# Score projection as 64x128 tiles on two row halves, four PSUM banks a round

## The chip, the cores and the metric

The kernel runs on one core of one Trainium2 chip. The time is the device time of one execution in microseconds; the kernel before took 1718.86 us, the median of three runs (1711.59 to 1719.67). In the profile, PE is the tensor engine (PEld its weight loads), DVE the vector engine, ACT the scalar engine, POOL the GpSimd engine and SP the engine that here issues DMAs and executes no-ops.

## The reference

The input is one sequence of 2048 tokens of 448 numbers. Two layers run over it, each an attention and a feed-forward part with a residual addition, all with the same weights:

```python
x = x + attention(layernorm(x))      # layer one
x = x + feed_forward(layernorm(x))
x = x + attention(layernorm(x))      # layer two
x = x + feed_forward(layernorm(x))

# attention: 64 segments of 32 tokens, one after the other, 16 heads of 256
mem = mem0                                        # 8 rows
for s in range(64):
    h = concat(mem, x[32 * s:32 * s + 32])        # 40 rows of 448
    q, k, v = h Wq, h Wk, h Wv                    # for each head
    p = softmax(mask(q k^T / 16))
    o = sum over heads of (p v) Wo
    mem = o[:8]                                   # goes into the next segment
    out[s] = o[8:]

# feed_forward: relu(x W_gate) * (x W_up), then W_down; 448 -> 1792 -> 448
```

The memory rows make the segments of one attention a chain: segment s + 1 can't start before segment s has its output.

## The kernel before

**Folded weights.** At the start `score_weights` multiplies Wk and Wq of each head into one 448 x 448 matrix, so that the scores of a head are h M h^T. It lies in `M_sb` (the first 384 of the 448 contracted rows, as three blocks of 128 partitions) and `MT_sb` (the last 64 rows). `value_weights` folds Wv and Wo in the same way into `B_sb` and `BT_sb`.

**Two chains.** Layer one (chain C1) and layer two (C2) run interleaved, C2 five segments behind (`LAG`). There are 69 steps; step g does segment g of C1 and segment g - 5 of C2. So 59 steps hold both chains and ten hold one. The activations are kept transposed in `hTr`: slots 0 to 2 hold 128 rows each, slots 3 and 4 both stand for the last 64 rows. Slot 3 has them in partitions 0 to 63 and zeros below, slot 4 in partitions 64 to 127 and zeros above.

**A step**, in the order in which PE gets it:

1. The score projection G = M^T h (L320 to L337). It has 56 column tiles of 128, and 40 columns of h for each chain, so 80 with both. For each tile four matmuls follow one another, three on `M_sb` and one on `MT_sb`, each a full 128 x 128 array. `MT_sb` holds two heads' tails, one in each half of the partitions, and the zeros in slot 3 or 4 switch the other off. Six tiles fill a PSUM bank; ACT and DVE take turns in copying a bank to G (L333).
2. The scores (L353) in `S_ps`, which has two banks of its own. The first half of its matmuls reads tiles 0 to 27 of G, the second half tiles 28 to 55.
3. The softmax on DVE and ACT (L358 to L374), while PE multiplies the memory and token rows by the folded value weights (`values`, L265). `values` works already on 64 x 32 tiles of two row halves: each half fills its own banks, and a no-op on SP (L268) holds half 0 back from a bank that half 1 is still adding to.
4. The weighted sum (`AT_ps`, L421), its memory rows copied to `mb` (L427), transposed (L163) and put into `hTr` for the next step (L434, L435); last, the tokens' rows are added to the residual in `x_ring` (L446, one addition for each chain).

**PSUM.** All other tiles come from `bank`, which hands out six banks in turn. A tile's first writer waits until the bank's last reader is done:

```python
n_bank[0] += 1
return psum.tile(shape, dt, tag=f"b{n_bank[0] % 6}", name=name)
```

**The order around it** is written by hand. A plan for each step (chosen by g mod 4, called r) puts pieces of other work at named places: G0, G4, G6 and G9 in and behind the projection, P behind the softmax weights' transposes, A, B and T behind the weighted sum. A block of 128 tokens is normalized (`Norm`) once four segments of it are done, transposed (`turn`), and its feed-forward goes into a queue of seven `gate_up` blocks of 16 matmuls and one `down`. `fill` takes from that queue; the elementwise ends of the blocks wait in `owed` until `settle()` or a later `fill` puts them out. With r = 0 layer one's feed-forward runs seven blocks at G9 (between projection and scores) and `down` at P; layer two's blocks are spread over P, B and T of the next steps. Stores and reloads of `x_ring` are put off to the start of a later step (`deferred`), on SP's queue.

Of the kernel before, what the change touches and what calls it, by code (L numbers as in the profile page):

```python
# [10 lines left out]
F32 = mybir.dt.float32  # L11
# [5 lines left out]
DM = 448  # L17
# [3 lines left out]
NGT = 56  # L21
# [3 lines left out]
L = MEM + SEG  # L25
# [17 lines left out]
def build_kernel(ctx, tc, A_x, A_mem0, A_Wq, A_Wk, A_Wv, A_Wo, B_W_gate, B_W_up, B_W_down, out,  # L43
                 ntiles=16, nseg=64):
    nc = tc.nc
    P = nc.NUM_PARTITIONS
# [20 lines left out]
    M_sb = glob.tile([P, 3, H * DM], BF)  # L67
    MT_sb = glob.tile([P, H * DM // 2], BF)
# [7 lines left out]
    def bank(shape, dt, name):  # L76

        n_bank[0] += 1
        return psum.tile(shape, dt, tag=f"b{n_bank[0] % 6}", name=name)
# [78 lines left out]
    def transposed(xn, rows):  # L158

        tps = bank([P, NSL, P], BF, "tps")  # L160
        for kd in range(NSL):
            lo = 320 if kd == 4 else kd * 128
            nc.tensor.transpose(tps[:, kd, 0:rows], xn[0:rows, lo:lo + 128], ident[0:rows, 0:rows])  # L163
        return tps

    def prep_x(c, blk, tps):

        src = tps[:, :, :].rearrange("p k (s t) -> p s k t", t=SEG)
        s0 = (4 * blk + c.lag) % NR
        for a, b in ([(0, 4)] if s0 + 4 <= NR else [(0, NR - s0), (NR - s0, 4)]):  # L170
            r = slice((s0 + a) % NR, (s0 + a) % NR + b - a)
            nc.vector.tensor_copy(hTr[:, r, 0:4, c.cid, 0:SEG], src[:, a:b, 0:4])
            nc.scalar.copy(hTr[64:128, r, 4, c.cid, 0:SEG], src[64:128, a:b, 4])

    def set_mem0(c):
        r = c.lag % NR
        nc.vector.tensor_copy(hTr[:, r, :, c.cid, SEG:L], mem0T[:])  # L177
        lo = SEG - 2 * MEM + MEM * c.cid
        nc.gpsimd.tensor_copy(memTp[c.lag % 2][:, :, lo:lo + MEM], mem0T[:])
# [4 lines left out]
    def settle():  # L184

        while owed:
            owed.pop(0)()
# [55 lines left out]
    def fill(cid, n):  # L243
        for _ in range(n):
            if ffn_q[cid]:
                while len(owed) > 1:
                    owed.pop(0)()
                ffn_q[cid].popleft()()

    def after(later, earlier):  # L250
        tc.add_manual_dep(later.ins, earlier.ins.name, SYNC, reason="one row half leaves a bank before the other enters")

    def values(lhsT, dst, evac, between=lambda: None):
# [24 lines left out]
        for slot in range(14):  # L278
            for r in range(2):
                chunk(r, *order[r][slot])  # L280
            if slot in (10, 13):
                for g4 in ((0, 1) if slot == 10 else (2, 3)):
                    evac[g4](dst[:, g4, :], ps[g4][:, 0:DM])  # L283
                if slot == 10:
                    between()

    prev_vom = [None]
    cp_a = nc.scalar.copy
    cp_v = nc.vector.tensor_copy
# [12 lines left out]
    def step(g, plan):  # L302

        chains = [c for c in (C1, C2) if 0 <= g - c.lag < nseg]
        both = len(chains) == 2
        rg = g % NR
        c0, c1 = chains[0].cid, chains[-1].cid + 1
        NP = L * (c1 - c0)
# [3 lines left out]
        hT = hTr[:, rg]  # L312

        def at_place(name):
            for f in plan.get(name, []):
                f()
# [1 line left out]
        for _ in range(len(deferred)):  # L318
            deferred.popleft()()
        G = p_vo.tile([P, NGT, 2, L], BF, tag="G", name="G")  # L320
        per_bank = 480 // NP
        for bb, t0 in enumerate(range(0, NGT, per_bank)):
            n = min(per_bank, NGT - t0)
            ps = bank([P, 512], F32, "gps")
            for t in range(t0, t0 + n):
                p7, u = divmod(t, 7)
                q7 = 7 * (p7 // 2) + u
                for kd in range(4):
                    w = M_sb[:, kd, t * 128:(t + 1) * 128] if kd < 3 else MT_sb[:, q7 * 128:(q7 + 1) * 128]
                    nc.tensor.matmul(ps[:, (t - t0) * NP:(t - t0 + 1) * NP], w,  # L330
                                     hT[:, kd if kd < 3 else 3 + p7 % 2, c0:c1, :],
                                     start=(kd == 0), stop=(kd == 3))
            (cp_a if bb % 2 == 0 else cp_v)(  # L333
                G[:, t0:t0 + n, c0:c1, :], ps[:, 0:n * NP].rearrange("p (m c t) -> p m c t", m=n, t=L))
            if bb == 0:
                settle()
            at_place(f"G{(t0 * 80 // 480)}" if both else f"G{bb * 2}")  # L337
        at_place("G9" if not both else "-")
        settle()

        S_ps = S_next[0] if S_next[0] is not None else mask_scores(g)
# [1 line left out]
        for bb in range(2):  # L343
            r4 = slice(4 * bb, 4 * bb + 4)
            for sl in range(NSL):
                for c in chains:
                    o = S_ps[c.rb:c.rb + L, bb, 0:8 * L].rearrange("p (r e k) -> p r e k", e=2, k=L)
                    if sl < 3:
                        rhs = Gv[:, r4, sl:sl + 5:4, c.cid, :]
                    else:  # L350
                        rhs = Gv[:, r4, 3, c.cid, :]
                        o = o[:, :, sl - 3, :]
                    nc.tensor.matmul(o, hT[:, sl, c.cid, :], rhs, start=False, stop=(sl == NSL - 1),  # L353
                                     tile_position=(0, c.rb), skip_group_check=True)
# [5 lines left out]
        nc.vector.tensor_tensor(se[RR].rearrange("p (b h) k -> p b h k", b=2), S3,  # L360
                                mx[RR].unsqueeze(3).to_broadcast([nr, 2, 8, L]), op=ALU.subtract)
        nc.scalar.activation(se[RR], se[RR], AF.Exp, scale=SCALE)  # L362
        ssum = p_soft.tile([P, H], F32, tag="ssum")
        rs = p_soft.tile([P, H], F32, tag="rs")
        Px, Pm = PXM[g % 2]
# [51 lines left out]
        for k in range(8):  # L417
            for c in chains:
# [3 lines left out]
                                 start=(k == 0), stop=(k == 7), tile_position=(0, c.rb), skip_group_check=True)  # L422
        at_place("A")
        nxt = [c for c in chains if g + 1 - c.lag < nseg]
        for c in nxt:
            rows = slice(c.rb + SEG, c.rb + L)
# [26 lines left out]
    def load_T(n, i, tag):  # L453
        t = bp.tile([P, 8, DM], BF, tag=tag, name=f"w{n}")
        nc.sync.dma_start_transpose(t[:], srcs[n][:, 1024 * i:1024 * (i + 1)])
        return t
# [3 lines left out]
    def copy_out(dst, src):  # L460
        flip[0] ^= 1
        if flip[0]:
            nc.scalar.copy(dst, src)
        else:
            nc.vector.tensor_copy(dst, src)

    def product(dst, lt, rt, hh, lo, n):
        for t in range(2):
            nc.tensor.matmul(dst, lt[:, 2 * hh + t, lo:lo + n], rt[:, 2 * hh + t, :],  # L469
                             start=(t == 0), stop=(t == 1))  # L470

    def store_M(dst, odd, ps):
        if not odd:
            copy_out(dst[:, 0:448], ps)
        else:
            copy_out(dst[:, 512:896], ps[:, 0:384])
            copy_out(dst[:, 448:512], ps[:, 384:448])

    def score_weights():
        for i in range(4):  # L480
            wk = load_T("k", i, "wa")
            wq = load_T("q", i, "wb")
            for hh in range(4):
                o = 896 * ((4 * i + hh) // 2)
                for mt in range(3):
                    ps = bank([P, 512], F32, "wps")
                    product(ps[:, 0:DM], wk, wq, hh, 128 * mt, 128)
                    store_M(M_sb[:, mt, o:o + 896], hh % 2, ps[:, 0:DM])
            for e in range(2):
                ps = bank([P, 512], F32, "wps")  # L490
                for side in range(2):
                    product(ps[64 * side:64 * side + 64, 0:DM], wk, wq, 2 * side + e, 384, 64)
                store_M(MT_sb[:, 896 * i:896 * i + 896], e, ps[:, 0:DM])

    def value_weights():
        for i in range(4):
# [32 lines left out]
    for t in range(2):  # L529
        prep_x(C1, t, transposed(Norm(t).apply(), P))  # L530
    nc.gpsimd.tensor_copy(memTp[0][:, :, 0:16], hTr[:, 1, :, 0, 0:16])
    score_weights()

    for g in range(nsteps):
        gb, r = divmod(g, 4)
        if g == LAG:
            set_mem0(C2)
        plan = {}
        hold = {}

        def put(place, f):
            plan.setdefault(place, []).append(f)

        def norm_at(key, t, first, second):
            put(first, lambda: hold.__setitem__(key, Norm(t)))
            put(second, lambda: hold.__setitem__(key, hold[key].apply()))

        if r == 0:
            if 0 <= gb - 1 < ntiles:
                f1 = FFN(C1, gb - 1)  # L550
                norm_at("f", gb - 1, "G0", "G4")
                put("G6", lambda: f1.turn(hold["f"]))
                put("G9", lambda: fill(0, 7))
                put("P", lambda: fill(0, 1))
                put("P", settle)
                norm_at("c2", gb - 1, "P", "A")
                put("B", lambda: hold.__setitem__("c2", transposed(hold["c2"], P)))
                put("B", lambda: prep_x(C2, gb - 1, hold["c2"]))
            put("B", lambda: fill(1, 1))
        elif r == 1:  # L560
            if 0 <= gb - 2 < ntiles:
                f2 = FFN(C2, gb - 2)
                norm_at("f", gb - 2, "G0", "G4")
                put("G6", lambda: f2.turn(hold["f"]))
            for place in "PBT":
                put(place, lambda: fill(1, 1))
        elif r == 2:
            if gb + 2 < ntiles:
                norm_at("c1", gb + 2, "G0", "G4")
                put("G6", lambda: prep_x(C1, gb + 2, transposed(hold["c1"], P)))  # L570
            for place in "BT":
                put(place, lambda: fill(1, 1))
        else:
            for place in "PB":
                put(place, lambda: fill(1, 1))
        step(g, plan)
    fill(0, 20)
    fill(1, 20)
# [61 lines left out]
```

## Time and profile before

| | |
|---|---|
| median of three runs | 1718.86 us |
| the profiled execution | 1715.13 us, span 1713.4 us |
| mean granted clock of TensorE | 0.992 |
| PE busy | 1634.1 us, 95% |
| DVE, ACT, POOL busy | 988.0, 633.0, 138.3 us |
| projection matmuls (L330) | 15456, 202 ns each with 80 columns |
| G copied by ACT | 559 ns for 480 columns, 426 ns for 320 |
| G copied by DVE | 651 ns for 480 columns, 325 ns for 160 |
| DMA | 28.83 MB, 17 GB/s |

A matmul's duration in the profile holds its way through the array, and matmuls overlap; what one costs in a run is the distance between two starts. In a list of groups a row is: line, engine, operation, tile written <- tiles read, shape and count, then busy time and mean duration, then idle time before it and what ended it. In a timeline a row is: start, time until the end of the merged rows, engine, line and operation, count, and the idle time before it with what ended it. In a table of windows, each engine has its busy time and the count of its instructions, then come the granted clock, the share of DMA and GB/s.

The set-up takes the first 47 us, the first step with both chains starts its projection at 181 us. From there on steps of one kind agree: from projection to projection 32.4 us with r = 0, 21.3 with r = 1, 22.7 with r = 2 and 20.2 with r = 3 (medians).

### The profile page before, as it was taken

What the parts mean: (1) busy time and instruction counts of PE and PEld (TensorE: products, weight loads), DVE (VectorE), ACT (ScalarE), POOL (GpSimd) and SP (SyncE); (2) the same over time, 40 slices, a digit from 0 to 9 for tenths busy, and PEclk for the clock granted to TensorE, in tenths of its full rate; (3) what the DMA queues carried; (4) which work ended last, traced back from release to release, by engine and by line L of the source; (5) the groups of instructions that cost most, each with busy time, mean ns of one, the idle gap of its engine ahead of it and who ended that gap; (6) DMA issues with size and microseconds to landing.
All of it is one profiled execution on the core that took longest, in us unless ns stands there. A gap on an engine that the chain in (4) does not pass through costs nothing.

```text
span 1713.4 us, 88473 instructions
## 1 busy us (share of the span) xinstructions
PE 1634.1 (95%) x41883; PEld 1252.6 (73%) x41883; DVE 988.0 (58%) x1916; ACT 633.0 (37%) x1365; POOL 138.3 (8%) x373
## 2 busy tenths in 40 slices
PE   5889999999999999999999999999999999999998
PEld 2457677777778787777778777787778777787775
DVE  4534556655665656655665556555566556555544
ACT  3423333333334333333334343333333343333332
POOL 1000001000000000000000000010000000010000
PEclk9989999999999999999999999999999999999999
DMA  8730000000000000000000000000000000000000
GB/s 186 175 115 3 3 3 4 4 3 9 3 9 3 6 6 6 7 3 9 3 9 4 6 7 6 6 3 9 3 9 4 6 4 6 4 3 7 3 7 8
DMA packets 55259, 28.83 MB, mean 17 GB/s; under 512 B 44008, under 2 KB 54000, under 8 KB 54896
## 3 DMA queue, kind: packets, MB, share of 16 engines
q1 hardware_dynamic: 54880, 23.17, 5.4%
q8 instruction: 327, 5.36, 1.3%
q14 instruction: 36, 0.29, 0.1%
q10 hardware_dynamic: 16, 0.01, 0.0%
HBM read 10.33 MB, written 1.84 MB: 7 GB/s over the span
## 4 chain that ended last, share of the span: by engine, by line
PE 86%; DVE 8%; ACT 2%; issue 1%; DMA 1%; POOL 1%; SPq 0%; POOLq 0%; ACTq 0%
PE gps L330 31%; PE vps L265 21%; PE gu L209 10%; PE AT_ps L421 7%; PE dps L224 5%; PE S_ps L353 5%; PE tps L163 3%; PE wps L469 2%; DVE Px L370 2%; PE PT_ps L409 2%; DVE mb L427 2%; ACT mb L427 2%; DVE ssum L373 1%; PE S_ps L296 1%; DVE Pm L370 1%
## 5 line engine op out<-in xcount | busy, mean ns | idle before, releaser
L330 PE MATMUL gps<-hTr,M_sb 128*128 128x80 bf16 (+1 forms) x11592 | 546.7, 199 | 0.9 <-DVE hTr L177 0.7
L330 PEld LDWEIGHTS <-M_sb 128*128 128x128 bf16 x11592 | 538.3, 100 | 10.4 <-issue 8.9
L330 PE MATMUL gps<-hTr,MT_sb 128*128 128x80 bf16 (+1 forms) x3864 | 538.7, 199 | 2.6 <-issue 2.6
L330 PEld LDWEIGHTS <-MT_sb 128*128 128x128 bf16 x3864 | 384.7, 100 | 2.7 <-issue 2.7
L333 ACT CAST G<-gps 128x480 bf16<-128x480 f32 (+1 forms) x325 | 180.4, 555 | 367.5 <-PE gps L330 367.5
L265 PE MATMUL vps<-B_sb,hTr 64*32 64x448 bf16 x9216 | 275.2, 349 | 1.0 <-issue 0.7
L333 DVE CAST G<-gps 128x480 bf16<-128x480 f32 x315 | 184.2, 590 | 142.0 <-PE gps L330 140.9
L265 PEld LDWEIGHTS <-hTr 64*32 64x32 bf16 x10752 | 158.1, 93 | 101.2 <-issue 11.7
L209 PE MATMUL gu<-xnT,Wgu 128*128 128x128 bf16 x2688 | 215.3, 220 | 0.7 <-ACT xnT L197 0.7
L209 PEld LDWEIGHTS <-Wgu 128*128 128x128 bf16 x2688 | 187.6, 98 | 19.3 <-issue 17.9
L209 PE MATMUL gu<-xnT,WguT 128*128 128x128 bf16 x896 | 196.8, 220 | 0.0
L265 PE MATMUL vps<-B_sb,memTp 64*32 64x448 bf16 x6624 | 195.3, 350 | 1.5 <-SPq L268 1.5
L215 DVE SCALAR_TENSOR_TENSOR hh<-gu,ut 128x256 bf16<-128x256 f32 x224 | 92.3, 423 | 141.9 <-ACT ut L214 141.9
L283 ACT CAST vox<-vps 128x448 bf16<-128x448 f32 x192 | 101.6, 532 | 168.4 <-PE vps L265 166.2
L265 PEld LDWEIGHTS <-memTp 64*32 64x32 bf16 x7728 | 105.8, 92 | 70.6 <-SPq L268 1.9
L283 DVE CAST vox<-vps 128x448 bf16<-128x448 f32 x192 | 113.4, 623 | 48.8 <-PE vps L265 47.5
L362 ACT ACTIVATE se<-se 104x640 f32<-104x640 f32 (+1 forms) x69 | 50.8, 737 | 185.9 <-DVE se L360 185.9
L421 PE MATMUL AT_ps<-VOm,PT 128*40 128x448 bf16 x640 | 111.6, 356 | 2.0 <-ACT PT L410 1.4
L214 ACT CAST ut<-gu 128x256 bf16<-128x256 f32 x224 | 80.8, 376 | 82.9 <-PE gu L209 76.0
L370 POOL TENSOR_TENSOR Pm<-se,rs 40x128 bf16<-40x128 f32 x88 | 52.1, 592 | 732.3 <-DVE rs L374 529.2
L283 ACT CAST VOm<-vps 128x448 bf16<-128x448 f32 x207 | 95.7, 533 | 3.9 <-PE vps L265 3.8
L358 DVE TENSOR_REDUCE mx<-S_ps 104x16 f32<-104x640 f32 (+1 forms) x69 | 56.9, 824 | 59.8 <-PE S_ps L353 59.8
(87 smaller groups left out, 1724.3 us busy)
## 6 DMA issues: line engine op xcount, KB each, us to landing
wo<-in_A_Wo_dram SPq DMA_DIRECT2D x4, 896.0 KB, 5.9
out_dram<-x_ring SPq DMA_DIRECT2D x16, 112.0 KB, 1.7
Wd_sb<-in_B_W_down_dram SPq DMA_DIRECT2D x1, 1568.0 KB
x_ring<-in_A_x_dram SPq DMA_DIRECT2D x12, 112.0 KB, 2.3
Wgu<-in_B_W_gate_dram SPq DMA_DIRECT2D x1, 1344.0 KB, 6.3
Wgu<-in_B_W_up_dram SPq DMA_DIRECT2D x1, 1344.0 KB, 11.9
x_ring<-in_A_x_dram SPq DMA_DIRECT2D x1, 448.0 KB, 6.8
WguT<-in_B_W_gate_dram SPq DMA_DIRECT2D x1, 224.0 KB, 6.8
```

Source lines behind the costliest of these rows:

```text
L209: nc.tensor.matmul(ps[:, i, ff], w, self.xnT[:, kd if kd < 3 else 3 + i], start=(kd == 0), stop=(kd == 3))
L214: nc.scalar.copy(ut[:], ps[:, 1])
L215: nc.vector.scalar_tensor_tensor(out=self.hh[:, f:f + 2, :], in0=ps[:, 0], scalar=0.0, in1=ut[:], op0=ALU.max, op1=ALU.mult)
L224: nc.tensor.matmul(ps[:, 0:DM], self.hh[:, f, :], Wd_sb[:, f, :], start=(f == 0), stop=(f == FT - 1))
L265: mm = nc.tensor.matmul(ps[g4][32 * hq:32 * hq + 32, 0:DM], lhsT(rows, i if i < 3 else 3 + r), w, start=first, stop=final, tile_position=( ...
L283: evac[g4](dst[:, g4, :], ps[g4][:, 0:DM])
L330: nc.tensor.matmul(ps[:, (t - t0) * NP:(t - t0 + 1) * NP], w, hT[:, kd if kd < 3 else 3 + p7 % 2, c0:c1, :], start=(kd == 0), stop=(kd == 3))
L333: (cp_a if bb % 2 == 0 else cp_v)(G[:, t0:t0 + n, c0:c1, :], ps[:, 0:n * NP].rearrange("p (m c t) -> p m c t", m=n, t=L))
L353: nc.tensor.matmul(o, hT[:, sl, c.cid, :], rhs, start=False, stop=(sl == NSL - 1), tile_position=(0, c.rb), skip_group_check=True)
L370: eng.tensor_tensor(dst, se[rr, :, lo:hi], rs[rr, :].unsqueeze(2).to_broadcast([n, H, hi - lo]), op=ALU.mult)
L421: nc.tensor.matmul(at[c.rb:c.rb + L, 0:DM], PT[:, gg, c.rb:c.rb + L], rhs, start=(k == 0), stop=(k == 7), tile_position=(0, c.rb), skip_gr ...
L427: (cp_a if c is chains[0] else cp_v)(mb[rows, 0:DM], at[rows, 0:DM])
```

## The change

The projection works on half-height tiles. The 448 contracted rows are now seven pieces of 64; three full blocks give each row half (partitions 0 to 63 and 64 to 127) three pieces, and the tail is one more, in the half that holds it. `project` takes n tiles from each of four groups at a time. Tiles 0 to 27 belong to half 0, 28 to 55 to half 1, and each half has two banks for its own tiles. First each half does four pieces of its own tiles (three blocks and the tail), bank 0 and then bank 1, the two halves' matmuls alternating. Then each goes over to the other half's banks and adds its three pieces there. Half 0 may enter a bank of half 1 only when half 1 has left it: a no-op on SP waits for the last matmul of half 1 there, and half 0's first matmul waits for the no-op. After that ACT copies half 0's bank to G and DVE half 1's.

With both chains there are three such rounds (5, 5 and 4 tiles a bank, 400 or 320 columns), with one chain two (7 tiles, 280 columns). The places G0 and G4 come behind the first round and the last but one, G6 and G9 behind the last. What `owed` holds is put out ahead of the rounds, not behind the first bank.

`MT_sb` is laid out to match: the tails of heads 0 to 7 in partitions 0 to 63, of heads 8 to 15 in partitions 64 to 127, each head written by a product of its own.

Layer one's seven `gate_up` blocks (r = 0) move from G9 to a new place, S, behind the scores and the exponential, with a `settle` behind them.

```diff
+    def project(G, hT, c0, c1, NP, q0, n):
+        t0s = [[q0, q0 + n], [28 + q0, 28 + q0 + n]]
+        ps = [[bank([P, 512], F32, "gps") for b in range(2)] for r in range(2)]
+        gates = {}
+
+        def run(r, own, b):
+            h = r if own else 1 - r
+            rows = slice(64 * r, 64 * r + 64)
+            for i in range(n):
+                t = t0s[h][b] + i
+                for kd in range(4 if own else 3):
+                    w = M_sb[rows, kd, t * 128:(t + 1) * 128] if kd < 3 else MT_sb[rows, (t % 28) * 128:(t % 28 + 1) * 128]
+                    mm = nc.tensor.matmul(ps[h][b][:, i * NP:(i + 1) * NP], w,
+                                          hT[rows, kd if kd < 3 else 3 + r, c0:c1, :],
+                                          start=own and i == 0 and kd == 0, stop=not own and kd == 2,
+                                          tile_position=(64 * r, 0), skip_group_check=True)
+                    if r == 0 and not own and i == 0 and kd == 0:
+                        after(mm, gates[b])
+                    yield mm
+
+        for own in (True, False):
+            for b in range(2):
+                for _, mm in zip(run(0, own, b), run(1, own, b)):
+                    pass
+                if own:
+                    gates[b] = nc.sync.nop(hint="row halves")
+                    after(gates[b], mm)
+                else:
+                    for h, cp in ((0, cp_a), (1, cp_v)):
+                        cp(G[:, t0s[h][b]:t0s[h][b] + n, c0:c1, :],
+                           ps[h][b][:, 0:n * NP].rearrange("p (m c t) -> p m c t", m=n, t=L))
...
-        per_bank = 480 // NP
-        for bb, t0 in enumerate(range(0, NGT, per_bank)):
...
-            if bb == 0:
-                settle()
-            at_place(f"G{(t0 * 80 // 480)}" if both else f"G{bb * 2}")
-        at_place("G9" if not both else "-")
+        quads = [(0, 5), (10, 5), (20, 4)] if both else [(0, 7), (14, 7)]
+        settle()
+        for q, (q0, n) in enumerate(quads):
+            project(G, hT, c0, c1, NP, q0, n)
+            at_place("G0" if q == 0 else "-")
+            at_place("G4" if q == len(quads) - 2 else "-")
+        at_place("G6")
+        at_place("G9")
         settle()
...
         nc.scalar.activation(se[RR], se[RR], AF.Exp, scale=SCALE)
+        at_place("S")
...
-            for e in range(2):
+            rows = slice(64 * (i // 2), 64 * (i // 2) + 64)
+            for hh in range(4):
+                o = 896 * (2 * (i % 2) + hh // 2)
                 ps = bank([P, 512], F32, "wps")
-                for side in range(2):
-                    product(ps[64 * side:64 * side + 64, 0:DM], wk, wq, 2 * side + e, 384, 64)
-                store_M(MT_sb[:, 896 * i:896 * i + 896], e, ps[:, 0:DM])
+                product(ps[rows, 0:DM], wk, wq, hh, 384, 64)
+                store_M(MT_sb[rows, o:o + 896], hh % 2, ps[rows, 0:DM])
...
-                put("G9", lambda: fill(0, 7))
+                put("S", lambda: fill(0, 7))
+                put("S", settle)
```

More of the change, by code (lines that the diff above doesn't have):

```diff
@@ L320, in step @@
         G = p_vo.tile([P, NGT, 2, L], BF, tag="G", name="G")
-        per_bank = 480 // NP
-        for bb, t0 in enumerate(range(0, NGT, per_bank)):
[L323 to L334, printed above, removed]
-            if bb == 0:
-                settle()
-            at_place(f"G{(t0 * 80 // 480)}" if both else f"G{bb * 2}")
-        at_place("G9" if not both else "-")
+        quads = [(0, 5), (10, 5), (20, 4)] if both else [(0, 7), (14, 7)]
[6 more added lines that the diff above has]
+        at_place("G9")
         settle()
```

## The prediction

> **What bounds the kernel now.** I read the page's totals first, then the chain that ended last, the groups by shape, and timelines of single steps.
>
> ```profile
> span 1713.4 us, 88473 instructions
> PE 1634.1 (95%) x41883; PEld 1252.6 (73%) x41883; DVE 988.0 (58%) x1916; ACT 633.0 (37%) x1365; POOL 138.3 (8%) x373
> ...
> PE 86%; DVE 8%; ACT 2%; issue 1%; DMA 1%; POOL 1%; SPq 0%; POOLq 0%; ACTq 0%
> PE gps L330 31%; PE vps L265 21%; PE gu L209 10%; PE AT_ps L421 7%; PE dps L224 5%; PE S_ps L353 5%; PE tps L163 3%; PE wps L469 2%; DVE Px L370 2%; PE PT_ps L409 2%; DVE mb L427 2%; ACT mb L427 2%; DVE ssum L373 1%; PE S_ps L296 1%; DVE Pm L370 1%
> ```
>
> PE is the path, and the score projection (L330) is its largest piece. So any time that PE waits here is time of the kernel. Next, what a matmul costs: windows inside the values stage and the projection of one step, then a timeline of a projection with one chain.
>
> ```profile
> 1005.30:1010.30 5.00, 5.00 (x217) 3.21 (x223) 4.28 (x7) 2.03 (x4) 0.55 (x1) 1.00 0.02 3
> 996.00:1003.90 7.90, 7.90 (x225) 7.90 (x223) 3.77 (x7) 2.79 (x6) 0.00 (x0) 1.00 0.02 5
> ```
>
> ```profile
> 126.16 0.18 PE L330 MATMUL gps<-hTr,MT_sb 128*128 128x40 bf16 x1
> ...
> 126.27 0.18 PE L330 MATMUL gps<-hTr,MT_sb 128*128 128x40 bf16 x1
> ```
>
> In the windows PE's column is busy time and count. Projection: first to last of 224 starts is 7.99 us, so 35.8 ns each and 8.02 us in all. Values (64x32 tiles on both row halves, 448 columns): 217 in 5.00 us, 23 ns each, so eight share some 190 ns: row halves do run side by side. With 40 columns four matmuls take 0.10 to 0.11 us (126.16 to 126.27): 25 to 26 ns, hardly less than 36, so something other than columns binds there.
>
> **The matmuls.** 448 rows are 3.5 blocks of 128, and the old loop pays four: 56 x 4 = 224. The new one has 56 x 7 = 392 half-height matmuls, 196 pairs. If a pair takes what one full matmul takes (36.0 ns, the 35.8 and a little for the second start), a step takes 7.06 us: 0.96 less. Over the 59 steps with both chains: -57 us. The other end: halves take turns at the 25 ns of the 40-column rows, 50 ns a pair, 9.80 us: +1.78 a step, +105 us. I take the first: in the values stage eight loads and eight matmuls of two row halves start within 25 ns, so the 25 looks like the limit of one tile, not of the engine. But those tiles' weights are 32 columns wide, these are 128.
>
> [...]
>
> **Where the new rounds wait.** `bank()` hands out six PSUM banks in turn. The old projection fills one at a time and comes to a just-used one late. A round of `project` takes four at once: ps[0][0], ps[0][1], ps[1][0], ps[1][1] are what was handed out six, five, four and three calls before the last four of the round. The second instruction of a round already writes ps[1][0].
>
> *Opening.* Counting calls back from a step's end: in steps with g mod 4 = 1, 2, 3 ps[1][0] is the bank of `AT_ps` (after it came three calls: transposes, gates or down, memory transposes); with g mod 4 = 0 only two came after, and it is ps[1][1]. AT_ps is read last by the two residual additions (L446), on DVE behind the hTr copy:
>
> ```profile
> 1048.33 0.19 DVE L434 COPY hTr<-tps 128x64 bf16<-128x64 bf16 x1 [1.60 <-PE tps L163]
> 1048.44 1.24 DVE L446 TENSOR_TENSOR x_ring<-AT_ps,x_ring 32x448 bf16<-32x448 f32 x2
> 1048.56 0.17 ACT L435 COPY hTr<-tps 64x16 bf16<-64x16 bf16 x1 [1.53 <-DVE hTr L434]
> 1048.58 0.27 PE L330 MATMUL gps<-hTr,M_sb 128*128 128x80 bf16 x3
> ```
>
> The additions end 1.10 us after the projection's first start here (g = 41). Other steps of the timeline: 0.50 for g mod 4 = 2 and 3, where feed-forward matmuls stand in front, 1.25 for 0. DVE to PE takes 0.06 (DVE's copy ends 1048.52, PE starts 1048.58). Waits: 1.16 in 15 steps, 0.56 in 30, and in 14 steps 1.25 + 0.06 less the 20 pairs ahead of ps[1][1], 0.72: 0.59. Sum 17.4 + 16.8 + 8.3 = +42 us. Queued behind the waiting matmul is all of PE's step; the old order reached this bank 1.7 us later, which hid it. Moving settle() ahead of the rounds puts the owed products in front of the first evacuations: their bank, ps[1][1] where g mod 4 = 2 or 3, is free some 1.0 us after the start (0.50 + 0.43 for L215) and wanted at 1.28: nothing.
>
> *Between rounds.* ps[1][0] of a round is ps[0][0] of the one before, which ACT empties only once half 1 has added its share; 15 pairs (0.54 us) follow. Evacuation starts 0.24 us after the last matmul's start (here 1003.67 to 1003.91), takes 0.49 for 400 columns (rows: 426 ns for 320, 559 for 480), and 0.06 back: 0.79, wanted after 16 pairs, 0.58. Wait 0.21, twice a step: +25 us.
>
> *Into the scores.* Before:
>
> ```profile
> 1056.84 0.20 PE L330 MATMUL gps<-hTr,MT_sb 128*128 128x80 bf16 x1
> 1056.97 1.27 PE L353 MATMUL S_ps<-G,hTr 128*40 128x320 bf16 x20
> 1057.08 0.32 DVE L333 CAST G<-gps 128x160 bf16<-128x160 f32 x1 [0.29 <-PE gps L330]
> ```
>
> The scores follow 0.13 us behind the last matmul, since their first half needs tiles 0 to 27, long evacuated; the late one is wanted only by the second half. In the new order tiles 24 to 27 leave in the last evacuation: 0.24 + 0.43 + 0.06 = 0.73 us, so +0.59. The five transposes that stood inside the projection (span 8.27 against 7.99) now stand in this gap: -0.28 in steps 0, 1, 2. Where g mod 4 = 0 the seven gate_up blocks covered this gap and no longer do; behind the scores they cost the same 6.2 us, plus one more change of tile shape, some 0.1 (feed-forward to AT_ps starts 0.15 apart against 0.056 in a run). Sums: 0.41 x 14 + 0.31 x 30 + 0.59 x 15 = +24 us. The move pays nothing back: in those steps the softmax was already hidden (PT_ps starts 0.28 behind the values, the least of all steps; 0.60 and 0.71 in the odd ones). Its owed products run on ACT and DVE while PE does values.
>
> *Gates.* The no-op waits for the last own matmul (0.20 to its end), about 0.15 on to SP and back: 0.35, against 0.54 us or more of other pairs in between. The values stage has the same distance and waits on it 3 times in 328. Cost nothing; without that cover 0.35 six times a step, 124 us. Output stores and their reloads stand on SP at a step's start, about 0.6 us each, ahead of gates that are wanted at 1.4 us.
>
> *Once.* In step 0 the no-ops stand on SP ahead of `value_weights`' loads. The first of these started at 39.93 us, during the set-up; now it waits for the last gate, some 52.5. The products that need it started at 57.34; loads took 9.1 us from issue to use later (64.44 to 73.59), so 61.6: +4. The extra tail copies (six a group, three before; 0.22 to 0.62 us each on two engines) show in the last group only, about 1 us, inside that. Bounds 0 and 12.6 (all of the delay). The ten one-chain steps gain 0.7 (28 x 25 ns) and wait about 0.9: +2.
>
> **Sum:** -57 + 42 + 25 + 24 + 4 + 2 = +40 us on 1715.13 (the profiled execution; span 1713.4, 1.7 us around it; the median of the runs shown is 3.7 us higher, 0.2%): 1755 us. Each bank wait could be off by 0.1 us, three to four a step: some 20 us either way, 1735 to 1775.
>
> **Rivals.**
> 1. *Halves don't pair*: the change does not do what it says, and 392 starts at 25 ns bind. +105, no wait between rounds (16 pairs are 0.80), openings 38, scores 24, 6 once: +173, 1888; at the values' 23.6 a start (eight per 189), +74 in place of 105, 1857. For: 25 ns at 40 columns. Against: the values stage.
> 2. *The bank waits don't bite*: faster. If the second half's first matmul found its bank free at openings and changes of round, 67 us go: -57 + 24 + 6 = -27, 1688. It decides below 0.3 us of bank wait a step (18 us in all), where I count 1.1. For: the projection shows 0.9 us of idle time in the whole trace, with the same six banks. Against: the order of calls and 1048.44 + 1.24.
> 3. *Only the openings are free*: -2, 1713, no change.
>
> **Chances.** 1755 case 0.60; halves don't pair 0.24 (and 0.03 worse than 1890); no bank waits 0.08; openings free 0.05. A measurement tells 0.5%, 8.6 us, from no change. From these: faster 0.09, same 0.08, slower 0.83. Range 1728 to 1888: the first case with its 20 us and a little, up to the second.
>
> **What would show it.** Right: in the two-chain steps, pairs 36 ns apart; PE stopping at its second projection matmul until L446 ends; 0.2 us twice later on, released by ACT's G; 0.73 us before S_ps; the first wv load near 52 us. Wrong: starts 25 ns apart throughout, or a projection of 7.1 us without gaps, or waits on SP.

## The result and the profile after

The changed kernel takes 1913.06 us (median of four runs, 1908.57 to 1915.02) against 1719.26 for the kernel before (four runs, 1711.59 to 1720.45): a ratio of 1.1137, 95% interval 1.1104 to 1.1171. Slower was right, the size was not: 40 us were predicted and some 194 came, and the time lies outside the range. In the two profiled executions the span goes from 1713.4 to 1911.7 us: +198.3 us to find.

The page's totals and the chain that ended last, of the kernel after:

```profile
span 1911.7 us, 112193 instructions
PE 1669.4 (87%) x53475; PEld 1230.4 (64%) x53475; DVE 1013.1 (53%) x2001; ACT 646.0 (34%) x1440; POOL 137.9 (7%) x373
...
PE 74%; DVE 10%; issue 8%; ACT 6%; DMA 1%; POOL 0%; SPq 0%; ACTq 0%; POOLq 0%
```

PE's busy time rose by 35 us, but its share fell from 95% to 87%, and the chain now holds 10% of DVE, 6% of ACT and 8% of "issue", time in which the engine waited for nothing that the profile shows; before, those were 8, 2 and 1. The list of waits says where (columns: who waited, for what, us in total, times, the longest):

```profile
PEld L301 <- issue: 154.9, 257, 2.1
PE gps L301 <- issue: 108.7, 127, 2.0
PE gps L301 <- DVE x_ring L471: 24.9, 57, 1.0
PE S_ps L377 <- ACT G L318: 15.9, 46, 0.5
```

The projection is L301 now, its copies to G L318, the scores L377 and the residual additions L471 (before: L330, L333, L353, L446). The last two lines are waits that the prediction priced. The first two are not in it at all.

A timeline at an opening (r = 3, where r is g mod 4; feed-forward stands in front), where the additions are read beside the second matmul:

```profile
1102.09 1.25 DVE L471 TENSOR_TENSOR x_ring<-AT_ps,x_ring 32x448 bf16<-32x448 f32 x2
1102.93 0.21 PE L301 MATMUL gps<-hTr,M_sb 64*128 64x80 bf16 x1
1103.40 0.28 PE L301 MATMUL gps<-hTr,M_sb 64*128 64x80 bf16 x5 [0.26 <-DVE x_ring L471]
```

One matmul starts at 1102.93, the next at 1103.40, 0.06 us after the additions end at 1103.34: the wait that was described, 0.47 us from start to start where 0.56 were counted. Further on in the same projection, timelines of three places:

```profile
1106.27 0.21 PE L301 MATMUL gps<-hTr,MT_sb 64*128 64x80 bf16 x2
1107.05 0.28 PE L301 MATMUL gps<-hTr,M_sb 64*128 64x80 bf16 x6 [0.57 <-issue]
1110.79 0.35 PE L301 MATMUL gps<-hTr,M_sb 64*128 64x80 bf16 x10 [1.28 <-issue]
```

PE stops before 1107.05 and before 1110.79, and no semaphore releases it. The weight loads stop too (the first line of the list of waits), so it is not a matmul that is held by its output. A window from the one restart to the other, of the projection alone (PE's busy time and count, then the loads', the granted clock, the share of DMA, GB/s):

```profile
1107.04:1110.78 3.74, 2.47 (x128) 2.33 (x128) 1.00 0.02 4
```

128 matmuls and 128 loads: exactly 256 instructions from gap to gap. They pass in 2.4 us, and then nothing passes for 1.3. This is no single case: of the 132 such gaps in this kernel's projections, 130 stand before a matmul whose number, counted from the start of the program, leaves the same remainder when divided by 128. The page's table of DMA queues has a queue for instructions (packets, MB, share of time), first of the kernel before, then of the kernel after:

```profile
q8 instruction: 327, 5.36, 1.3%
```

```profile
q8 instruction: 418, 6.85, 1.5%
```

6.85 MB in 418 packets are 16384 bytes each, and 418 x 256 = 107,008 is the number of PE's matmuls and loads (106,950). The kernel before has 327 packets for 83,766. So PE is fed in blocks of 256 instructions. In the trace's records of this queue, successive packets of the kernel after start no less than 3.25 us apart, a quarter of them within 3.5; before, the least is 3.32 and the median 4.57. A block of the new projection is used up in 64 pairs x 36 ns = 2.3 us. A block of the old one, at 35.8 ns for a load and a matmul, lasted 4.6.

Last, the way into the scores:

```profile
1112.81 0.43 PE L301 MATMUL gps<-hTr,M_sb 64*128 64x80 bf16 x14
1112.86 0.85 ACT L318 CAST G<-gps 128x320 bf16<-128x320 f32 x2 [1.27 <-PE gps L301]
1113.77 0.32 PE L377 MATMUL S_ps<-G,hTr 128*40 128x320 bf16 x2 [0.53 <-ACT G L318]
```

By distances between starts, the 59 two-chain projections account for the change so (only gaps over 120 ns count as gaps):

| part | before to after | predicted |
|---|---|---|
| matmuls, without the gaps | 469.6 to 413.7: -55.9 us | -57 |
| opening, released by L471 | +34.2 in 55 gaps | +42 |
| between rounds, released by ACT's G | +27.2 in 115 | +25 |
| into the scores: 0.13 to 0.74 each, less 0.28 for the transposes in 45 steps | +23.4 | +24 |
| SP's no-ops | +0.3 in 1 | 0 |
| **released by nothing** | **+95.2 in 110** | **none** |
| put down to a releaser that was done long before | +8.0 in 7 | none |
| values stages, between neighbouring matmuls | 375.0 to 385.1: +10.1 | none |

The seven stand at the same place of a block of 128 matmuls as the 110 above them, 0.1 to 1.2 us behind the instruction that the profile names (twice SP's no-op), so they belong with them. In the values stages it is the weight loads that wait for nothing shown, before and after:

```profile
PEld L265 <- issue: 12.1, 31, 0.7
```

```profile
PEld L265 <- issue: 30.9, 82, 1.7
```

The rows of the table sum to +142.5. Measured from the first two-chain projection to the last, the steps take +143.2. The ten one-chain steps and the set-up and end around them take +25.0 up to that point and +30.1 behind it, where +6 was predicted: 35.9 us in 22 more gaps that nothing released, some 8 from a lower clock (below), about 5 from the later loads of the value weights.

### The profile page after: what moved, and what is told of

It reads as the page before. It is cut to its first block, busy times and chain, and to the rows that moved or that the text cites. A ratio compares the mean times of both kernels' runs of the same rounds, so it can differ in the third digit from the quotient of the medians.

```text
span 1911.7 us, 112193 instructions
## 1 busy us (share of the span) xinstructions
PE 1669.4 (87%) x53475; PEld 1230.4 (64%) x53475; DVE 1013.1 (53%) x2001; ACT 646.0 (34%) x1440; POOL 137.9 (7%) x373
## 3 DMA queue, kind: packets, MB, share of 16 engines
q8 instruction: 418, 6.85, 1.5%
## 4 chain that ended last, share of the span: by engine, by line
PE 74%; DVE 10%; issue 8%; ACT 6%; DMA 1%; POOL 0%; SPq 0%; ACTq 0%; POOLq 0%
PE gps L301 24%; PE vps L265 21%; PE gu L209 8%; PE AT_ps L446 6%; PE S_ps L377 5%; PE dps L224 4%; ACT G L318 4%; DVE x_ring L471 4%; PE wps L494 3%; PE tps L163 2%; PE PT_ps L434 2%; DVE mb L452 2%; ACT mb L452 1%; DVE Px L395 1%; DVE ssum L398 1%
## 5 line engine op out<-in xcount | busy, mean ns | idle before, releaser
L301 PE MATMUL gps<-hTr,M_sb 64*128 64x80 bf16 (+1 forms) x23184 | 536.6, 196 | 141.6 <-issue 103.3
L301 PEld LDWEIGHTS <-M_sb 64*128 64x128 bf16 x23184 | 490.4, 97 | 192.2 <-issue 148.7
L318 DVE CAST G<-gps 128x400 bf16<-128x400 f32 (+2 forms) x394 | 204.7, 536 | 370.1 <-PE gps L301 369.6
L318 ACT CAST G<-gps 128x400 bf16<-128x400 f32 (+2 forms) x394 | 181.6, 462 | 508.1 <-PE gps L301 503.9
L301 PE MATMUL gps<-hTr,MT_sb 64*128 64x80 bf16 (+1 forms) x3864 | 290.1, 195 | 5.4 <-issue 5.4
L265 PE MATMUL vps<-B_sb,hTr 64*32 64x448 bf16 x9216 | 281.0, 350 | 4.5 <-issue 3.8
L301 PEld LDWEIGHTS <-MT_sb 64*128 64x128 bf16 x3864 | 222.4, 97 | 6.2 <-issue 6.2
L377 PE MATMUL S_ps<-G,hTr 128*40 128x320 bf16 (+1 forms) x1280 | 99.1, 284 | 19.1 <-ACT G L318 15.9
L446 PE MATMUL AT_ps<-VOm,PT 128*40 128x448 bf16 x640 | 110.7, 354 | 2.2 <-ACT PT L435 1.2
```

The lines of the kernel that those rows point to most:

```text
L265: mm = nc.tensor.matmul(ps[g4][32 * hq:32 * hq + 32, 0:DM], lhsT(rows, i if i < 3 else 3 + r), w, start=first, stop=final, tile_position=( ...
L301: mm = nc.tensor.matmul(ps[h][b][:, i * NP:(i + 1) * NP], w, hT[rows, kd if kd < 3 else 3 + r, c0:c1, :], start=own and i == 0 and kd == 0 ...
L318: cp(G[:, t0s[h][b]:t0s[h][b] + n, c0:c1, :], ps[h][b][:, 0:n * NP].rearrange("p (m c t) -> p m c t", m=n, t=L))
L446: nc.tensor.matmul(at[c.rb:c.rb + L, 0:DM], PT[:, gg, c.rb:c.rb + L], rhs, start=(k == 0), stop=(k == 7), tile_position=(0, c.rb), skip_gr ...
```

## The experiments

The theory, S in the expectations, is supply: a block of 256 PE instructions comes no faster than one in some 3.3 us, 12.9 ns an instruction, and code that uses them faster than that runs dry. The rivals that they name put the lost time on the array, on the starts of the halves or on the banks, and not on a count of instructions. The kernels whose range is given below ran four times, the others once.

**Only the first pass.** Each half adds its share to its own tiles alone, 224 matmuls a step in place of 392.

```
-                 start=own and i == 0 and kd == 0, stop=not own and kd == 2,
+                 start=own and i == 0 and kd == 0, stop=kd == 3,
-        for own in (True, False):
+        for own in (True,):
...
-                if own:
-                    gates[b] = nc.sync.nop(hint="row halves")
-                    after(gates[b], mm)
-                else:
+                if True:
```

> The changed kernel with the halves' second visit left out: each half adds its share to its own tiles only, so half of the scores' sums is missing, and there are no gates. 112 pairs a step in place of 196. Theory S (PE's instructions come in blocks of 256, one block in no less than 3.3 us, and 784 of them in a projection are too many): 84 pairs of 36 ns less are 178 us over 59 steps and some 20 over the ten short ones, and of the 130 us of gaps that nothing released more than half go too: about 1630 us. Rival P (halves don't pair, 25 ns a start): 168 starts x 25 ns x 59 = 248 us less: about 1665, starts evenly 25 ns apart, no gaps. Rival B (only bank waits, as predicted): 200 us less plus the 25 of the waits between rounds: 1690.

Measured: 1576.71 us (before on the same chip 1714.67). This kernel has 41,883 matmuls, exactly as many as the kernel before, and so as many instructions; the gaps that nothing released are still 45 us (47 of them), where the kernel before has 3.5 us of idle time before its projection matmuls. The number of instructions alone does not do it, then; their density does. The gaps fell from 131 us by 87, about the 85 in S's sum, but its total is 53 us too high: the waits between rounds fell too, by 20 us, the values stages became 10 shorter, and outside the two-chain steps the kernel lost some 23 us more than the matmuls and gaps that S counted there. The projection of r = 3 takes 5.11 us first start to last: 448 instructions at 9 ns are 4.03, and one gap is the rest. From the list of waits:

```profile
PE gps L301 <- issue: 36.1, 45, 4.6
```

**The first pass twice.** The same pairs in the same four banks, with no bank change more.

```
-        def run(r, own, b):
+        def run(r, own, b, again=0):
...
-        for own in (True, False):
+        for own, again in ((True, 0), (True, 1), (False, 0)):
...
+                if own and not again:
+                    continue
```

> The changed kernel with each half's own pass done twice (the second adds the same again): 112 pairs and 448 instructions of PE more a step. Theory S: the projection is bound by the supply of instructions, 448 x 13.3 ns = 6.0 us a step, +411 us over 69 steps: about 2320. Theory B (array time decides, 36 ns a pair): 4.0 us a step, +266 us: about 2180.

Measured: 2347.01 us. The projection of r = 3 grows from 9.6 to 15.99 us: 6.3 for 448 more instructions, 14 ns each where the pairs by themselves cost 9. The gaps grow to 283.6 us in 247. This speaks for S and against an array price, which would be 4.0 us.

```profile
PE gps L301 <- issue: 240.4, 243, 1.9
```

**Old loops, a no-op for each matmul of the projection and of the values stage.** It was to raise the number of instructions and leave the matmuls alone; the line stands in both loops.

```
+                    nc.tensor.nop(hint="pad")
```

> The kernel before with one no-op of PE behind each matmul of the projection and of the values stage: 492 instructions more a step, no arithmetic added. Theory S: 672 instructions in the projection at 13.3 ns need 8.9 us against 8.0, and 336 in a values stage 4.5 against 2.65, less what lies ready at the start of each: +100 to +230 us, in gaps of about 1 us that nothing releases, at every 256 instructions. Rival (the supply is no limit): below +20 us.

Measured: 3943.89 us, 2229 more. It settles nothing: the matmuls of both loops now start 90 ns apart (36 and 23 before), 30 ns an instruction, and instruction packets (460 in the span of 3942.1 us) are 5.9 us apart at the least and 8.5 in the median, so nothing ran short of them. 2229 us over 33,936 no-ops are 66 ns each, with the clock fallen to 0.845.

**Full height for three blocks, pairs for the tails only.** The old loop's three 128-row blocks stay, and only the half blocks run two side by side: 168 matmuls of 128 rows and 28 pairs a step, 448 instructions as before. Both halves' tiles share a round; `at_place` and the copies are spread between. (Two-chain steps; the one-chain ones keep the old loop.)

```
+            def full(k, r, last):
+                for j, t in enumerate(rounds[k][r]):
+                    for kd in range(3):
+                        mm(k, r, j, kd, slice(0, P), kd, M_sb[:, kd, t * 128:(t + 1) * 128], last and kd == 2)
+            def tails(k, last):
+                for j in range(sizes[k]):
+                    for r in range(2):
...
+                        rows = slice(64 * r, 64 * r + 64)
+                        mm(k, r, j, 3, rows, 3 + r, MT_sb[rows, q7 * 128:(q7 + 1) * 128], last)
...
```

> The kernel before, with the projection's three full blocks left as 128x128 matmuls and only the 64-row tails paired on the two row halves: 168 + 28 pairs, 224 matmuls and 448 instructions a step as before, two banks a round in five rounds ordered so that the tile shape changes four times. No half changes banks, no gates. Theory S: nothing starves, 196 x 36 ns = 7.06 us and four changes of shape at 0.1: -0.5 us a step, -30 us: about 1687. Rival P (halves take turns at 25 ns): -0.1 us a step, about 1710. If changing shape costs 0.2: about 1710 as well, with the starts of the pairs still 36 ns apart.

Measured: 1683.36 us (1677.09 to 1687.63), 0.981 of the kernel before, interval 0.9777 to 0.9843: faster than both kernels, if not clearly by 2%. A window over one projection with r = 3, then a group of the kernel before and two of this one by shape:

```profile
1072.60:1080.10 7.50, 7.50 (x228) 7.24 (x225) 4.20 (x11) 2.70 (x8) 0.02 (x1) 1.00 0.01 2
```

```profile
L330 PE MATMUL gps<-hTr,M_sb 128*128 128x80 bf16 x9912 | 486.4, 202 | 0.9 <-DVE hTr L177 0.7
```

```profile
L354 PE MATMUL gps<-hTr,M_sb 128*128 128x80 bf16 x9912 | 385.3, 202 | 0.9 <-DVE hTr L177 0.7
L354 PE MATMUL gps<-hTr,MT_sb 64*128 64x80 bf16 x3304 | 79.7, 199 | 0.0
```

PE is busy for the whole of its window and waits for nothing. The projection of r = 3 takes 7.41 us first start to last against 7.99: 196 x 36 ns = 7.06, and the rest is four changes of tile shape at some 0.1 us (at each, the next start comes 130 to 135 ns behind the last, in place of 36). So the saving that the change was after exists, at the price the prediction gave it, with the instructions at 448 a step.

**The change again, and half the columns.** Two kernels on one chip, the kernel after as it is and one whose two-chain projection streams one chain's 40 columns in place of 80.

> The changed kernel unaltered, for comparison on the same chip with the runs beside it: 1913 us, as before.

```
-                                          hT[rows, kd if kd < 3 else 3 + r, c0:c1, :],
+                                          hT[rows, kd if kd < 3 else 3 + r, c0, :],
...
```

> The changed kernel with half the columns in each projection matmul (only the first chain's 40 of 80; the copy to G writes them to both chains). Every instruction stays, the array has half to do. Theory S (blocks of 256 instructions, one in 3.3 us or more): 784 instructions still take what they took, 0 to -40 us against 1913. Theory B (array time and bank waits): a pair falls from 36 to at most 25 ns (the one-chain rows), 196 x 11 ns x 59 = 127 us less: about 1785.

Measured: 1917.38 us (1914.74 to 1920.5) and 1982.22. With half of the array's work in the projection the kernel was slower. First to last start, the four kinds of projection take 9.56, 9.93, 9.55 and 9.46 us, within 0.6 of what they take in the same chip's kernel after (9.7, 10.5, 9.7, 9.7), though a pair now takes 27 ns in place of 36; the gaps that nothing released grew from 138 to 194 us in 136, and with the waits for G's copies (27 to 42 us) they took up most of the 97 us that the array gave back. That is what S says of the projection. What neither theory had is the total: the granted clock falls from 0.974 to 0.872, and stages beside the projection take longer: the matmuls of the scores are busy for 155.1 us, 404 ns each, where the kernel after has 99.1 us and 284 ns. What lowered the clock, this run does not show. A window over one projection and the list of waits:

```profile
921.28:930.14 8.86, 5.99 (x392) 5.49 (x392) 3.43 (x8) 2.27 (x6) 0.00 (x0) 0.93 0.02 5
```

```profile
PE gps L301 <- issue: 177.8, 139, 2.8
```

PE is busy for 5.99 of 8.86 us; in a window over the projection at 1102.93 of the kernel after it was 7.96 of 10.17.

**Without the residual additions.** The wait at the opening goes.

```
-            nc.vector.tensor_tensor(xrows, at[c.rb:c.rb + SEG, 0:DM], xrows, op=ALU.add)
+            pass
```

> The changed kernel with the attention's residual additions left out, so that the bank of AT_ps is free when the projection opens. Theory B (each wait adds to the sum): the 34 us of waits at the openings go, 1879. Theory S: while PE waits there the next block of instructions comes in, so the gaps later on grow by what the openings give up: less than half of it is gained, 1896 to 1913.

Measured: 1886.97 us (1886.11 to 1889.83), 30.4 less than the kernel after beside it. Here S was drawn too simply: it said that a block would be fetched during the wait, and that a gap would take the wait's place. The gaps hold 136 us here and 138 beside it, and almost all of the 34.2 us came back. That fits an opening at which all the instructions that PE can hold are already there, so that waiting brings in nothing more; it was not seen directly.

```profile
PE gps L301 <- issue: 112.7, 125, 2.5
```

**Feed-forward back at its old place.** Layer one's seven gate_up blocks stand at G9 again, ahead of the scores.

```
-                put("S", lambda: fill(0, 7))
-                put("S", settle)
+                put("G9", lambda: fill(0, 7))
```

> The changed kernel with layer one's seven gate_up blocks back at G9, between projection and scores. They cover the wait of the scores for the last evacuation in the 14 steps with g mod 4 = 0: 0.6 us each, -8 us, 1905; a little more if PE's instructions catch up during the 6.2 us. If the place behind the scores hid the softmax, it would be slower than 1913.

Measured: 1926.35 us (1924.64 to 1930.11), 9 more than the kernel after beside it, where 8 less were expected. Steps with g mod 4 = 0 take 35.11 us against 34.62. A timeline of the place:

```profile
1143.24 0.45 PE L163 MATMUL tps<-ident,xn 128*128 128x128 bf16 x5
1143.73 0.59 ACT L197 COPY xnT<-tps 128x512 bf16<-128x512 bf16 x1
1144.35 0.23 DVE L198 COPY xnT<-tps 64x128 bf16<-64x128 bf16 x1 [0.54 <-ACT xnT L197]
1144.37 0.33 PE L209 MATMUL gu<-xnT,Wgu 128*128 128x128 bf16 x3 [0.67 <-ACT xnT L197]
```

The five transposes stand behind the rounds now, directly ahead of gate_up, which needs what they make: 0.67 us of waiting for the copy. In the whole trace there are 17 such waits, 11.5 us in all, and in the kernel after beside it one. Behind the scores the copy has the scores' time. Once the rounds are taken four banks at a time, moving the feed-forward is worth 9 us.

**A block that lasts longer.** Last, the inverse of half the columns: 120 columns in place of 80, the surplus multiplied and not used. Both kernels of this pair transpose the weights of the set-up on PE and not by DMA; the first is the partner alone.

```
-        nc.sync.dma_start_transpose(t[:], srcs[n][:, 1024 * i:1024 * (i + 1)])
+                    nc.tensor.transpose(tp[:, 112 * k:112 * k + 112], raw[0:112, k, 128 * c:128 * c + 128], ident[0:112, 0:112])
...
```

> The changed kernel with the weights of the set-up transposed by PE instead of by the DMA (plain loads, 384 transposes): the partner of the next run. The set-up changes by some tens of us either way; from the first two-chain step on the steps are those of the changed kernel, 24.7 us each on the mean.

```
+                    if c1 - c0 == 2:
+                        lo = min(slot * 80, NSL * 80 - 120)
+                        rhs, wide = hT[rows, :, :, :].rearrange("p k c t -> p (k c t)")[:, lo:lo + 120], 120
...
```

> The same, with half as many columns again in each projection matmul of the two-chain steps (120 in place of 80; the extra 40 read what lies beside them and land on the next tile's columns, so the sums are not the reference's). [...] With 80 columns a block lasts 64 x 36 ns = 2.3 us, which leaves gaps of 1.0 us; with 120 it lasts 64 x 52.5 = 3.36 us, which leaves none. A projection with g mod 4 = 3 goes from 9.6 to 196 x 52.5 ns + 0.4 of opening = 10.7 us, +65 us over 59 steps and a little more. Rival (each block costs its gap whatever runs): +3.2 us a step, 12.9 us, +190.

Measured: 1952.56 and 1994.17 us. (For the same edit without the transposes on PE, which has no result, +90 us had been expected.) The groups by shape, first of the partner, then of the wide one (busy time, mean, then idle time before them and what ended it):

```profile
L301 PE MATMUL gps<-hTr,M_sb 64*128 64x80 bf16 x19824 | 476.8, 198 | 100.9 <-issue 67.4 <-DVE x_ring L471 24.1 <-DVE xn L154 0.8
```

```profile
L307 PE MATMUL gps<-hTr,M_sb 64*128 64x120 bf16 x19824 | 632.0, 213 | 21.6 <-DVE x_ring L476 19.1 <-DVE hTr L177 0.7 <-issue 0.5
```

With half as many columns again, the gaps are gone: 67.4 us of idle time to 0.5 in this group, and by the starts 105 us in 114 gaps to 3 us in 13 over the two-chain projections; only the one-chain steps, which stayed as they were, keep theirs (34). A pair now takes 53 ns, a block 3.4 us, just more than the 3.3. The projection of r = 3 goes from 9.75 to 10.72 us, as S has it, and the waits between rounds are gone too, since 16 pairs are 0.84 us against 0.79 for the copy. The two-chain projections together grew by 58 us (582 to 640), where S had summed 65, and the values stages, whose loads now wait 19.5 us for nothing shown in place of 38.7, became 16 us shorter: so the total rose by 42 us. With half the columns, the gaps grew; with half as many more, they vanished; the number of instructions never moved. Of the causes weighed here, only a limit on their supply does both.

How far ahead PE holds instructions was not seen. An estimate: not far. 418 blocks at 3.3 us are 1379 of 1911.7 us, so a large store, filled in the slower stages, should have covered most of the projections' gaps, and 131 us of them lay open.

## Why the prediction was wrong, point by point

**The matmuls.** The term was array time, 196 x 36.0 ns = 7.06 us a step, and as such it was right: without the gaps the pairs run 36 ns apart (two thirds of the starts 1 to 6 and 29 to 39 ns apart, the rest 9 to 26), 413.7 us against 469.6. The step that failed stands behind that: that a step would take those 7.06 us. It priced each pair and never asked whether PE could be handed 784 instructions in that time, 9 ns each. The page had the row for it, the instruction queue's 327 packets, about one every 5.2 us of the span, and it was not read. The limit itself stood in the records of that queue, whose least distance was 3.32 us: at 13 ns each, 784 instructions are an estimated 10.2 us, a little less if some lie ready at the start. The values window that was used as evidence (217 matmuls in 5.00 us, 11.5 ns an instruction) was itself under the 12.9. It holds no gap, but over the whole kernel before the loads of that stage wait 12.1 us for nothing shown, and ten pauses of its matmuls (0.27 to 0.58 us from start to start) all stand at one place of the block of 128. The missing term is 95.2 us in the two-chain steps, 103 with the seven gaps that are put down to others, and 35.9 in the one-chain ones.

The other end that was weighed, halves that take turns at the 25 ns of the 40-column rows, was set aside rightly: 392 starts at 25 ns are not what binds, since a third of the starts come 1 to 6 ns behind the last. Its 9.80 us a step is nevertheless what the projections took (9.56 to 10.27 first start to last, the medians of the four kinds). A number can be met by another cause: in the kernel with half the columns 25 ns a start and the supply would again give the same step, and only the gaps at every 256th instruction part them.

**The opening:** right in place and cause, 34.2 us against 42; for r = 2 and 3 the additions end 0.40 us after the start, not 0.50. Taking the additions away gave 30.4 back.

**Between rounds:** right, 27.2 against 25. **Into the scores:** right, 0.74 against 0.73 for the gap. **Gates:** right, 0.3 us in one of them.

**"The move pays nothing back":** wrong. It was judged against the old order; in the new one it covers the copy of the transposes, 9 us.

**Set-up:** right where it was followed. The first value weights load starts at 53.98 (some 52.5 predicted), and the next step's projection starts 4.8 us later, +4 predicted:

```profile
53.98 3.39 SPq L480 DMA_TRANSPOSE wv<-in_A_Wv_dram  x1
```

**One-chain steps:** wrong, +2 against some 50 with the end of the kernel. With 40 columns the pairs ask for instructions faster still (27 ns a pair, 7 an instruction), and for part of the time PE runs at half clock; that being held up is what lowers it is not shown. A window over the scores of such a step shows it in the clock column: 1.90 us, where before 1.20 sufficed at a clock of 1.00 (first line before, second after).

```profile
128.30:129.50 1.20, 1.12 (x11) 0.77 (x10) 0.00 (x0) 0.69 (x2) 0.00 (x0) 1.00 0.00 0
```

```profile
140.40:142.30 1.90, 1.90 (x10) 1.25 (x10) 0.42 (x1) 0.26 (x1) 0.00 (x0) 0.50 0.00 0
```

**The rivals.** "Halves don't pair" had the nearest totals, 1857 and 1888, and the wrong reason: the halves pair. The bank waits bite, so the other two fell. Of the signs named as telling against the forecast, neither starts 25 ns apart nor a smooth 7.1 us nor, beyond 0.3 us, waits on SP appeared: the list had no place for idle time that nothing releases.

**What stays open:** why a block takes 3.3 us or more to arrive. In the records of the kernel after, the next packet starts 1.14 us (median) after PE has gone on behind a gap, takes 1.0, and PE goes on 1.4 us after its end: one packet follows the other, but what fills the times between them is not known. And how many instructions are ready ahead at any moment is inferred from the gaps and not seen.

## What to carry to other kernels

Price a stream of small instructions twice: by what the array takes for each, and by how many there are, here 256 PE instructions (128 loads and 128 matmuls) in 3.3 us at best. The larger of the two comes near the time: 784 instructions are 10.1 us where 9.6 to 10.3 were measured, 448 are 5.8 where it was 5.1 (that the difference lay ready at the start is an estimate, it was not seen). Cutting a tile in two to fill the array doubles the count, so cut only where rows are really wasted: the tails alone in pairs gave 0.981, everything in pairs 1.114. In a profile, idle time that nothing releases, a multiple of 256 instructions apart and in matmuls and loads alike, was the sign of it here.

## What the runs showed of the hardware

- At 9 ns an instruction PE stalled at the ends of blocks of 256: 110 gaps of 0.9 us on the mean in the two-chain projections of the kernel after, which hold some 181 blocks. At 13 ns (120 columns) 13 gaps of 3 us in all were left. Instruction packets started no less than 3.32 us apart in the kernel before and 3.25 in the kernel after, where PE went on 1.1 to 1.6 us after one had ended.
- Less work was slower in one run: half the columns left the projections nearly as long as they were, the granted clock was 0.872 in place of 0.974, and the time 65 us longer.
- Pairs of 64x128 tiles with 80 columns came 36 ns apart in the kernel after; in the kernel with full height for three blocks a change between full-height and half-height tiles cost some 0.1 us (130 to 135 ns to the next start in place of 36); with a no-op behind each, the matmuls of the old loops started 90 ns apart.
